# A retention layer and a spatial-gating MLP in one kernel: the order of the first loads, the split of a group's loads, and the engine of one residue

## The chip, the cores and the metric

The kernel runs on one core of one Trainium2 chip. The time is device microseconds (us) of that core for one execution; lower is better. Engines are named as in the profile: PE is TensorE (PEld its weight load), DVE is VectorE, ACT is ScalarE, POOL is GpSimd, SP is SyncE, which here only issues transfers (DMAs).

## The reference

Inputs q, k, v have 4 batches, 8 heads, 768 positions and 64 features per head. The first half is a retention layer, a linear attention with a decay per head; the second an MLP with spatial gating on its output x (4 x 768 x 512):

```
state = gamma[h] * state + outer(k_t, v_t)          # 64 x 64 for each batch and head
y_t   = scale * q_t @ state
x     = y laid out as (batch, position, 8*64)
h     = relu(x @ w_in)                              # 512 -> 1024, u and v are its halves
v_n   = (v - mean(v)) / sqrt(var(v) + 1e-6)         # over the 512 features
v_s   = w_spatial @ v_n + b_spatial                 # over the 768 positions
out   = (u * v_s) @ w_out                           # 512 -> 512
```

## The kernel before, in words

**Precision.** The large products are made from two halves of each operand: a high part, rounded to the fast fp32r format, and a low part, the residue (whole minus high). Each product is three matmuls: high x high, high x low, low x high (`split3`, L348). So every operand needs a rounded copy (an ACT cast) and a residue. A residue is made in one of two ways: by `residue` (L125), one subtraction on DVE or POOL; or by `residue_unit` (L146), in which PE multiplies the whole by the identity, subtracts the high part by a product with minus the identity, all in PSUM, and ACT copies the result out.

**Groups.** The sequence is cut into chunks of 128 positions: 6 chunks in each of 4 batches, 24 groups. `load_group` (G, L224) issues four requests for a group: two of 256 KB that bring q and v (tile `qv`, three buffers), one of 512 KB that brings the keys twice, transposed for the scores and natural for the state update (tile `kk`, two buffers), and one of 256 KB with the decays by which the output is multiplied (tile `qd`, two buffers). POOL then multiplies the values by a decay (L241). `ret_set` (S, L265) of group g updates the state with the natural keys of g and makes the scores of group g+1 with the transposed keys of g+1; in the first batch the state is summed in PSUM (tile `total`) and ACT copies it out (L263); DVE masks the scores (L316). `ret_out` (X, L318) makes the group's output on PE, DVE multiplies it by the decays (tile `xf`, L342), ACT rounds it (L345), POOL makes its residue.

**MLP.** `mlp_v` (V, L359) makes v for a chunk, ACT its relu, DVE mean and variance (`bn_stats`, `bn_aggr`, L380 and L381), and POOL three tiny operations of 128 x 1: add epsilon, the power -0.5, minus mean times that (L382, L383, L385). `mlp_norm` (N, L388) normalises on ACT (L391), rounds on ACT (L392) and makes the residue `vnl`: with `residue_unit` (PE and ACT, tile `run`) for the first UNIT_NORM = 6 chunks, that is the first batch, with DVE afterwards. `item` (I, L472) is one of 8 units of a batch: the u products of the next unit (`mlp_u`), the spatial product (`mlp_spatial`, tile `sp`, which needs all six chunks of v_n of the batch), and the output product of the unit before (`mlp_out`, tile `o`), whose fourth unit writes three outputs to HBM from SP.

**Weights.** `load_double` (L) brings a block of 512 KB of a weight that comes as words of 64 bits, `split_double` (C, L168) splits it with six operations of ACT and DVE and then PE (first four blocks) or POOL. `load_spatial` (K) brings w_spatial, two requests of 768 KB (K0, K2) and four of 192 KB (K4, K5), and `split_spatial` (W) rounds a half row block on ACT and makes its residue on PE and ACT (six) or DVE (six).

**Order.** Four strings name the order in which this work is written: START, FIRST (batch 0's items, with batch 1's retention), REST (twice) and LAST. A number is a block, chunk or group; in FIRST and REST a group number counts from the batch. Within the text the build's scheduler places instructions on each engine by its own estimate of when their inputs are there; an engine then takes its list strictly in that order. Three things are pinned to the written order: all loads on SP's queue (`load`, L122; a load also stays behind an output request written just before it), loads issued by ACT (from the tenth weight block), and, after START, all matmuls. Waits of a request (for a buffer to come free) hold everything behind it on SP.

Of the kernel before, what the change touches and what calls it, by code (L numbers as in the profile page):

```python
# [9 lines left out]
F32 = mybir.dt.float32  # L10
# [6 lines left out]
ALU = mybir.AluOpType  # L17
# [9 lines left out]


START = (
    "v m e L0 G0 C0 L1 L2 S-1 C1 G1 L3 C2 S0 X0 G2 C3 L4 L5 S1 X1 K0 V0 C4 G3 S2 X2 K2 V1 C5 N0 G4 L6 "  # L30
    "S3 X3 V2 N1 G5 W00 W10 K4 K5 S4 X4 V3 N2 W20 W30 B V4 N3 L7 U5 X5 W40 W50 N4 V5 G6 N5 L8"
)
FIRST = (
    "C6 L9 I0 C7 W01 L10 C8 I1 G7 W11 W21 Z5 L11 C9 I2 S6 W31 G8 C10 I3 X6 S7 W41 W51 G9 C11 "
    "I4 X7 S8 G10 I5 X8 S9 G11 I6 X9 S10 G12 V0 V1 I7 X10 S11 N0 V2 N1 V3 N2 G13 X11 V4 N3 V5 N4 O7 "
    "N5"
)
REST = (
    "S0 I0 G2 X0 S1 I1 G3 X1 S2 I2 G4 X2 S3 I3 G5 X3 S4 I4 G6 X4 S5 I5 G7 X5 I6 "
    "V0 V1 I7 N0 V2 N1 V3 N2 V4 N3 V5 N4 O7 N5"  # L40
)
LAST = "I0 I1 I2 I3 I4 I5 I6 I7 O7"
# [4 lines left out]
FIRST_QUEUE = 9  # L47
UNIT_BLOCKS = 4
UNIT_SPATIAL = 6
UNIT_NORM = 6  # L50
RAW_BUFS = 3
KK_BUFS = 2
WARM_UP = 10
QD_BUFS = 2


@with_exitstack
def tile_retention_gmlp(
    ctx: ExitStack,
    tc: tile.TileContext,  # L60
    qv: bass.AP,
    kk: bass.AP,
    w_inv: bass.AP,
    w_inu: bass.AP,
    w_sp: bass.AP,
# [2 lines left out]
    mask: bass.AP,  # L68
    eye: bass.AP,
    vdecay: bass.AP,  # L70
    qdecay: bass.AP,
    out: bass.AP,
):
    nc = tc.nc
    P = 128
    B = out.shape[0]
    NG = kk.shape[0]
    NC = NG // B
    C = P // 2
    D = C  # L80
    NP = kk.shape[2] // (4 * D)
    S = NC * P
    KT = w_inv.shape[1]
    DM = KT * P
# [3 lines left out]
    EPS = 1e-6  # L88
# [3 lines left out]
    rpool = ctx.enter_context(tc.tile_pool(name="ret", bufs=2))  # L92
# [7 lines left out]
    minus_t = wpool.tile([P, P], F32R, name="minus_t")  # L100
    vd_t = wpool.tile([P, NC, 2, NP], F32, name="vd_t")
    bsp_t = wpool.tile([P, S], F32, name="bsp_t")
    mhalf = wpool.tile([P, 1], F32, name="mhalf")
    nc.gpsimd.memset(mhalf, -0.5)

# [11 lines left out]
    def mm(out, lhs, rhs, start, stop, pin=False, shared=False):  # L117
        ins = nc.tensor.matmul(out, lhs, rhs, start=start, stop=stop, skip_group_check=shared)  # L118
        if pin or pinned:
            tc.keep_in_program_order(ins)  # L120

    def load(dst, src):  # L122
        tc.keep_in_program_order(nc.sync.dma_start(dst, src))  # L123

    def residue(eng, out, whole, high):  # L125
        eng.tensor_tensor(out, whole, high.bitcast(F32), ALU.subtract)  # L126
# [19 lines left out]
    def residue_unit(out, high, name, *parts):  # L146

        n = out.shape[-1]
        ps = ps_o.tile([P, DM], F32, tag="o", name=f"ru{name}")
        for k, part in enumerate(parts):  # L150
            mm(ps[:, :n], eye_t, part, start=(k == 0), stop=False)
        mm(ps[:, :n], minus_t, high, start=False, stop=True)
        nc.scalar.copy(out, ps[:, :n])  # L153

    def load_double(i):

        if i >= len(doubles):
            return
        if i < 6:
            tag = ("vnh", "vnl")[i // 3]  # L160
            if i % 3 == 0:
                raws[tag] = mpool.tile([P, 3, DM], I64, tag=tag, name=f"raw{i}", bufs=1)
            raws[i] = raws[tag][:, i % 3]
        else:
            raws[i] = mpool.tile([P, DM], I64, tag="raw", name=f"raw{i}", bufs=RAW_BUFS)[:, :]
        (load if i < FIRST_QUEUE else load_weight)(raws[i], doubles[i][2])

    def split_double(i):  # L168
        hi, lo, _ = doubles[i]
        parts = raws.pop(i).bitcast(I32).rearrange("p (n w) -> p n w", w=2)  # L170
        low, top = parts[:, :, 0], parts[:, :, 1]
        a = rpool.tile([P, DM], F32, tag="xf", name=f"da{i}")
        f = mpool.tile([P, DM], F32, tag="u", name=f"df{i}", bufs=3)
        ai, fi = a[:, :].bitcast(I32), f[:, :].bitcast(I32)
        nc.scalar.activation(a, top.bitcast(F32), AF.Abs)
        nc.vector.tensor_scalar(a, a, TOP_MAX, TOP_MIN, ALU.min, ALU.max)
        nc.vector.tensor_scalar(ai, ai, 0x07FFFFFF, 3, ALU.bitwise_and, ALU.logical_shift_left)
        nc.vector.scalar_tensor_tensor(fi, top, -0x40000000, ai, ALU.bitwise_and, ALU.bitwise_or)  # L178
        nc.vector.tensor_scalar(ai, fi, -0x800000, None, ALU.bitwise_and)
        nc.vector.scalar_tensor_tensor(a, low.bitcast(U32), 2.0**-52, a, ALU.mult, ALU.mult)  # L180
        nc.scalar.copy(hi, f)
        if i < UNIT_BLOCKS:
            residue_unit(lo, hi, f"d{i}", f, a)
        else:
            residue(nc.gpsimd, f, f, hi)
            nc.gpsimd.tensor_tensor(lo, f, a, ALU.add)  # L186
# [30 lines left out]
    queries = {}  # L217
    keys = {}
    naturals = {}
    values = {}  # L220
    decays = {}
    xhalf = {}

    def load_group(g):  # L224
        if g >= NG:
            return

        t = rpool.tile([P, 4, 2, NP, C], F32, tag="qv", name=f"qv{g}", bufs=3)
        kt = rpool.tile([P, 2, 2, NP, C], F32, tag="kk", name=f"kk{g}", bufs=KK_BUFS)
        qd = rpool.tile([P, NP, P], F32, tag="qd", name=f"qd{g}", bufs=QD_BUFS)  # L230
        for r in range(2):
            rows = t[ROWS[r], 2 * r : 2 * r + 2]
            load(rows.rearrange("p s i h c -> p (s i h c)"), qv[g, r])
        load(kt[:, :, :, :, :].rearrange("p s i h c -> p (s i h c)"), kk[g])
        load(qd, qdecay[g % NC])
        queries[g], keys[g], naturals[g] = (t[:, 2], t[:, 1]), kt[:, 0], kt[:, 1]
        values[g], decays[g] = (t[:, 0], t[:, 3]), qd
        for r in range(2):
            vd = vd_t[ROWS[r], g % NC].unsqueeze(3).broadcast_to([D, 2, NP, D])
            w = values[g][r][ROWS[r]]  # L240
            nc.gpsimd.tensor_tensor(w, w, vd, ALU.mult)  # L241

    total = {}

    def ret_total(g, i, pin):

        if not total:
            total[0] = ps_o.tile([P, NP, D], F32, tag="o", name="total")
        w = values[g]
# [15 lines left out]
    def ret_set(g, scores=True, update=True):  # L265

        nxt = scores and g + 1 < NG
        upd = [update and g >= 0, update and g >= 0 and g % NC < NC - 1]  # L270
# [77 lines left out]
    def split3(pairs, ps):  # L348
        n = len(pairs)
        i = 0  # L350
        for (ah, al), (bh, bl) in pairs:
            for l, r in ((ah, bh), (ah, bl), (al, bh)):
                mm(ps, l, r, start=(i == 0), stop=(i == 3 * n - 1))
                i += 1
# [4 lines left out]
    def mlp_v(b, c):  # L359
        if c == 0:  # L360
            vn[b] = (
                mpool.tile([P, NC, DM], F32R, tag="vnh", name=f"vnh{b}", bufs=1),
                mpool.tile([P, NC, DM], F32R, tag="vnl", name=f"vnl{b}", bufs=1),
            )
        xh, xl = xhalf[b, c // TT]
        cols = slice((c % TT) * P, (c % TT) * P + P)
        ps = ps_m.tile([P, DM], F32, tag="m", name=f"v{b}_{c}")
        split3(
            [
                ((xh[:, k, cols], xl[:, k, cols]), (winv_h[:, k], winv_l[:, k]))  # L370
                for k in range(KT)
            ],
            ps,
        )
        v = mpool.tile([P, DM], F32, tag="v", bufs=3, name=f"vr{b}_{c}")
        st = mpool.tile([P, 6], F32, tag="bst", bufs=2, name=f"bst{b}_{c}")
        mv = mpool.tile([P, 2], F32, tag="mv", bufs=3, name=f"mv{b}_{c}")
        rs = mpool.tile([P, 1], F32, tag="rs", bufs=3, name=f"rs{b}_{c}")
        nc.scalar.activation(v, ps, AF.Relu)  # L379
        nc.vector.bn_stats(st, v)  # L380
        nc.vector.bn_aggr(mv, st)  # L381
        nc.gpsimd.tensor_scalar(rs, mv[:, 1:2], EPS, None, ALU.add)  # L382
        nc.gpsimd.tensor_tensor(rs, rs, mhalf, ALU.pow)  # L383
        nb = mpool.tile([P, 1], F32, tag="nb", bufs=3, name=f"nb{b}_{c}")
        nc.gpsimd.tensor_scalar(nb, mv[:, 0:1], rs, -1.0, ALU.mult, ALU.mult)  # L385
        norm[b, c] = (v, nb, rs)

    def mlp_norm(b, c):  # L388
        vh, vl = vn[b]
        v, nb, rs = norm.pop((b, c))  # L390
        nc.scalar.activation(v, v, AF.Identity, bias=nb, scale=rs)  # L391
        nc.scalar.copy(vh[:, c], v)  # L392
        if b * NC + c < UNIT_NORM:
            residue_unit(vl[:, c], vh[:, c], f"n{b}_{c}", v)
        else:
            residue(nc.vector, vl[:, c], v, vh[:, c])

    gate = {}
    us = {}
# [72 lines left out]
    def item(b, i):  # L472
# [11 lines left out]
        "U": lambda b, g, n: ret_set(g + n, scores=False),  # L484
        "X": lambda b, g, n: ret_out(g + n),
        "G": lambda b, g, n: load_group(g + n),
        "L": lambda b, g, n: load_double(n),
        "C": lambda b, g, n: split_double(n),
        "W": lambda b, g, n: split_spatial(n // 10, n % 10),
# [98 lines left out]
```

## Time and profile before

| | |
|---|---|
| median of 3 runs | 446.26 us (445.85 to 450.62) |
| the profiled execution | 446.94 us, of it 445.2 us from the first to the last instruction (the span) |
| mean granted TensorE clock | 0.967 of full speed |
| bytes moved | 47.51 MB, mean 107 GB/s |

The profile shows one execution. Busy time of an engine is the time covered by its instructions. In the views, a line `L118 PE MATMUL run<-vr,eye_t` is the matmul helper at line 118 that writes tile `run` from tiles `vr` and `eye_t`; at the end of a line of the order in time, `[4.15 <-ACT winv_w L153]` says that the engine had been idle for 4.15 us and that the last thing it waited for was ACT's instruction of line 153 that writes `winv_w`. A row of the table by stretches gives, for a stretch from A to B, busy time of each engine with its number of instructions, then the granted PE clock, the busy share of the DMA engines and GB/s.

The span has three parts: START up to about 97 us, where the first u product of batch 0 begins; the items of batch 0 (FIRST) up to about 200 us; and batches 1 to 3.

### The profile page before, as it was taken

To read this page: it belongs to the slowest core of one execution; us is meant where nothing else is said; L and a number is where in the kernel's file an instruction comes from. 1 tells how busy PE (TensorE), PEld (TensorE's weight loads), DVE (VectorE), ACT (ScalarE), POOL (GpSimd) and SP (SyncE) were. 2 spreads that over 40 slices of the span, in tenths; PEclk is the share of its full clock that TensorE was granted. 3 is DMA by queue.
4 is the path that set the end of the run, shared out by engine and by line. 5 is a ranking of instruction groups with operands and counts; after the bars stand their busy time and mean duration, and the time that the engine had idled before them with its cause. 6 is when DMAs were issued, how large, how long until landed. Compare 5 with 4: busy or idle time off the path is not lost.

```text
span 445.2 us, 9212 instructions
## 1 busy us (share of the span) xinstructions
PE 404.7 (91%) x3842; PEld 345.3 (78%) x3842; DVE 201.4 (45%) x385; ACT 143.2 (32%) x268; POOL 164.5 (37%) x196
## 2 busy tenths in 40 slices
PE   3886799849997999899999499999999999999996
PEld 1354567539896988679998398889899988999995
DVE  2764933525955565437555212455555124322122
ACT  2343765623222214352112012471113124610312
POOL 2133864535635444433452522325442223210100
PEclk9998899969998999989999699999999999999999
DMA  7965878301123453407451810036432000100101
GB/s 216 266 211 150 271 242 252 117 5 47 49 80 135 144 155 84 143 35 198 134 157 47 250 39 0 0 105 180 121 119 96 2 0 2 71 1 0 71 1 71
DMA packets 17561, 47.51 MB, mean 107 GB/s; under 512 B 2544, under 2 KB 3440, under 8 KB 17520
## 3 DMA queue, kind: packets, MB, share of 16 engines
q1 hardware_dynamic: 17088, 45.35, 33.6%
q10 hardware_dynamic: 432, 1.57, 1.1%
q8 instruction: 30, 0.49, 0.5%
q14 instruction: 11, 0.09, 0.1%
HBM read 40.62 MB, written 6.29 MB: 105 GB/s over the span
## 4 chain that ended last, share of the span: by engine, by line
PE 78%; DMA 7%; DVE 5%; POOL 4%; ACT 3%; issue 2%; SPq 1%; ACTq 0%; DVEq 0%; POOLq 0%
PE sp L118 22%; PE u L118 16%; PE o L118 15%; PE v L118 13%; PE s L118 5%; PE x L118 4%; DMA wst<-in_w_sp_dram 3%; PE rud L118 2%; DMA qv<-in_qv_dram 1%; DMA raw<-in_w_inv_dram 1%; PE run L118 1%; POOL qv L241 1%; DMA kk<-in_kk_dram 1%; SPq L123 1%; DVE df L178 1%
## 5 line engine op out<-in xcount | busy, mean ns | idle before, releaser
L241 POOL TENSOR_TENSOR qv<-qv,vd_t 64x512 f32<-64x512 f32 x48 | 51.1, 1064 | 79.6 <-DMA qv<-in_qv_dram 70.0
L118 PE MATMUL u<-xh,winu_w 128*128 128x384 f32 x256 | 72.9, 348 | 0.0
L126 POOL TENSOR_TENSOR gl<-t,gh 128x384 fp32r<-128x384 f32 x31 | 31.7, 1023 | 106.6 <-ACT gh L442 104.9
L118 PE MATMUL v<-winv_w,xh 128*128 128x512 f32 x192 | 63.5, 412 | 5.7 <-ACT winv_w L153 4.1
L118 PE MATMUL sp<-wsp_h,vnl 128*128 128x384 f32 x192 | 64.2, 334 | 0.0
L118 PE MATMUL sp<-wsp_h,vnh 128*128 128x384 f32 x192 | 64.2, 334 | 0.0
L118 PE MATMUL sp<-wsp_l,vnh 128*128 128x384 f32 x192 | 64.2, 334 | 0.0
L118 PE MATMUL o<-wout_w,gh 128*128 128x512 f32 x192 | 61.3, 400 | 2.5 <-POOL wout_w L186 2.5
L440 DVE TENSOR_TENSOR t<-sp,bsp_t 128x384 f32<-128x384 f32 (+1 forms) x34 | 17.9, 533 | 100.6 <-PE sp L118 100.6
L118 PEld LDWEIGHTS u<-xh,winu_w 128*128 128x128 f32 x256 | 48.0, 193 | 2.1 <-issue 0.5
L118 PEld LDWEIGHTS v<-winv_w,xh 128*128 128x128 f32 x192 | 36.6, 194 | 14.5 <-ACT winv_w L153 4.3
L442 ACT CAST gh<-t 128x384 fp32r<-128x384 f32 (+1 forms) x34 | 16.6, 493 | 92.4 <-DVE t L441 92.2
L316 DVE TENSOR_TENSOR qv<-s,mask_t 64x256 f32<-64x256 f32 x92 | 38.6, 420 | 11.6 <-PE s L118 10.4
L118 PE MATMUL u<-xl,winu_w 128*128 128x384 f32 x128 | 43.6, 341 | 0.0
L118 PEld LDWEIGHTS o<-wout_w,gh 128*128 128x128 f32 x192 | 36.3, 191 | 8.9 <-POOL wout_w L186 2.9
L126 POOL TENSOR_TENSOR xl<-xf,xh 128x512 fp32r<-128x512 f32 x24 | 31.8, 1323 | 30.3 <-ACT xh L345 30.2
L118 PE MATMUL v<-winv_w,xl 128*128 128x512 f32 x96 | 38.9, 406 | 0.8 <-POOL xl L126 0.6
L118 PE MATMUL o<-wout_w,gl 128*128 128x512 f32 x96 | 38.3, 399 | 0.0
L380 DVE BATCH_NORM_STATS2 bst<-vr 128x6 f32<-128x512 f32 x24 | 16.7, 694 | 46.1 <-ACT vr L379 46.1
L118 PEld LDWEIGHTS sp<-wsp_l,vnh 128*128 128x128 f32 x192 | 36.0, 188 | 0.2
L118 PEld LDWEIGHTS sp<-wsp_h,vnh 128*128 128x128 f32 x192 | 36.0, 188 | 0.2
L118 PEld LDWEIGHTS sp<-wsp_h,vnl 128*128 128x128 f32 x192 | 36.0, 188 | 0.0
(75 smaller groups left out, 557.1 us busy)
## 6 DMA issues: line engine op xcount, KB each, us to landing
qv<-in_qv_dram SPq DMA_DIRECT2D x48, 256.0 KB, 4.8
kk<-in_kk_dram SPq DMA_DIRECT2D x24, 512.0 KB, 4.7
qd<-in_qdecay_dram SPq DMA_DIRECT2D x24, 256.0 KB, 2.8
out_dram<-ot SPq DMA_DIRECT2D x23, 256.0 KB, 2.1
raw<-in_w_inv_dram SPq DMA_DIRECT2D x4, 512.0 KB, 8.6
raw<-in_w_inu_dram SPq DMA_DIRECT2D x4, 512.0 KB, 5.7
wst<-in_w_sp_dram SPq DMA_DIRECT2D x2, 768.0 KB, 7.3
raw<-in_w_out_dram ACTq DMA_DIRECT2D x3, 512.0 KB, 3.8
```

The source lines that it names most:

```text
L118: ins = nc.tensor.matmul(out, lhs, rhs, start=start, stop=stop, skip_group_check=shared)
L123: tc.keep_in_program_order(nc.sync.dma_start(dst, src))
L126: eng.tensor_tensor(out, whole, high.bitcast(F32), ALU.subtract)
L178: nc.vector.scalar_tensor_tensor(fi, top, -0x40000000, ai, ALU.bitwise_and, ALU.bitwise_or)
L241: nc.gpsimd.tensor_tensor(w, w, vd, ALU.mult)
L316: nc.vector.tensor_tensor(m[r][ROWS[r], i], ts[i][col, 0], mk, ALU.mult)
L380: nc.vector.bn_stats(st, v)
L440: nc.vector.tensor_tensor(t[:, c], pp[:, c], bsp_t[:, tc_], ALU.add)
L442: nc.scalar.copy(gh[:, c], t[:, c])
```

## The change

The keys are no longer one tile. The transposed keys (`kt`, 256 KB, two buffers) stay in `load_group`, and a new function brings natural keys and decays together in one request of 512 KB (`kd`, two buffers). The new action D is written behind the output X of the group two back, whose buffer it takes. In START the weight requests L3 to L8, and K0, K2, K4, K5 stand earlier than before with respect to the groups' requests that wait. The residue of the normalised chunks is made on DVE in all batches (UNIT_NORM is gone), and of the three tiny operations per chunk the first and the last move from POOL to DVE; the power stays on POOL.

```diff
 START = (
-    "v m e L0 G0 C0 L1 L2 S-1 C1 G1 L3 C2 S0 X0 G2 C3 L4 L5 S1 X1 K0 V0 C4 G3 S2 X2 K2 V1 C5 N0 G4 L6 "
-    "S3 X3 V2 N1 G5 W00 W10 K4 K5 S4 X4 V3 N2 W20 W30 B V4 N3 L7 U5 X5 W40 W50 N4 V5 G6 N5 L8"
+    "v m e L0 G0 D0 C0 L1 L2 S-1 C1 G1 L3 C2 L4 D1 S0 X0 C3 L5 G2 K0 K2 D2 G3 S1 X1 V0 C4 K4 K5 L6 "
+    "D3 G4 S2 X2 V1 C5 N0 B L7 D4 G5 S3 X3 V2 N1 W00 W10 L8 D5 S4 X4 V3 N2 W20 W30 V4 N3 U5 X5 "
+    "W40 W50 N4 V5 G6 D6 N5"
 )
 FIRST = (
-    "C6 L9 I0 C7 W01 L10 C8 I1 G7 W11 W21 Z5 L11 C9 I2 S6 W31 G8 C10 I3 X6 S7 W41 W51 G9 C11 "
-    "I4 X7 S8 G10 I5 X8 S9 G11 I6 X9 S10 G12 V0 V1 I7 X10 S11 N0 V2 N1 V3 N2 G13 X11 V4 N3 V5 N4 O7 "
-    "N5"
+    "C6 L9 I0 C7 W01 L10 C8 I1 G7 W11 W21 Z5 L11 C9 I2 S6 W31 D7 G8 C10 I3 X6 S7 W41 W51 D8 G9 C11 "
+    "I4 X7 S8 D9 G10 I5 X8 S9 D10 G11 I6 X9 S10 D11 G12 V0 V1 I7 X10 S11 D12 N0 V2 N1 V3 N2 G13 X11 "
+    "D13 V4 N3 V5 N4 O7 N5"
 )
 REST = (
-    "S0 I0 G2 X0 S1 I1 G3 X1 S2 I2 G4 X2 S3 I3 G5 X3 S4 I4 G6 X4 S5 I5 G7 X5 I6 "
+    "S0 I0 G2 X0 S1 D2 I1 G3 X1 S2 D3 I2 G4 X2 S3 D4 I3 G5 X3 S4 D5 I4 G6 X4 S5 D6 I5 G7 X5 D7 I6 "
     "V0 V1 I7 N0 V2 N1 V3 N2 V4 N3 V5 N4 O7 N5"
 )
...
         t = rpool.tile([P, 4, 2, NP, C], F32, tag="qv", name=f"qv{g}", bufs=3)
-        kt = rpool.tile([P, 2, 2, NP, C], F32, tag="kk", name=f"kk{g}", bufs=KK_BUFS)
-        qd = rpool.tile([P, NP, P], F32, tag="qd", name=f"qd{g}", bufs=QD_BUFS)
+        kt = rpool.tile([P, 2, NP, C], F32, tag="kt", name=f"kt{g}", bufs=2)
...
-        load(kt[:, :, :, :, :].rearrange("p s i h c -> p (s i h c)"), kk[g])
-        load(qd, qdecay[g % NC])
-        queries[g], keys[g], naturals[g] = (t[:, 2], t[:, 1]), kt[:, 0], kt[:, 1]
-        values[g], decays[g] = (t[:, 0], t[:, 3]), qd
+        load(kt, kT[g])
+        queries[g], keys[g] = (t[:, 2], t[:, 1]), kt
+        values[g] = (t[:, 0], t[:, 3])
...
+    def load_natural(g):
+        if g >= NG:
+            return
+        t = rpool.tile([P, 2, 2 * NP * C], F32, tag="kd", name=f"kd{g}", bufs=2)
+        load(t[:, :, :].rearrange("p s n -> p (s n)"), kd[g])
+        naturals[g] = t[:, 0].rearrange("p (i h d) -> p i h d", i=2, h=NP)
+        decays[g] = t[:, 1].rearrange("p (h n) -> p h n", h=NP)
...
-        nc.gpsimd.tensor_scalar(rs, mv[:, 1:2], EPS, None, ALU.add)
+        nc.vector.tensor_scalar(rs, mv[:, 1:2], EPS, None, ALU.add)
         nc.gpsimd.tensor_tensor(rs, rs, mhalf, ALU.pow)
         nb = mpool.tile([P, 1], F32, tag="nb", bufs=3, name=f"nb{b}_{c}")
-        nc.gpsimd.tensor_scalar(nb, mv[:, 0:1], rs, -1.0, ALU.mult, ALU.mult)
+        nc.vector.tensor_scalar(nb, mv[:, 0:1], rs, -1.0, ALU.mult, ALU.mult)
...
-        if b * NC + c < UNIT_NORM:
-            residue_unit(vl[:, c], vh[:, c], f"n{b}_{c}", v)
-        else:
-            residue(nc.vector, vl[:, c], v, vh[:, c])
+        residue(nc.vector, vl[:, c], v, vh[:, c])
```

The host lays `kT` and `kd` out to match; sizes and buffers of a group add up to the same bytes as before.

More of the change, by code (lines that the diff above doesn't have):

```diff
@@ L49 @@
 UNIT_SPATIAL = 6
-UNIT_NORM = 6
 RAW_BUFS = 3
-KK_BUFS = 2
 WARM_UP = 10
-QD_BUFS = 2
 @with_exitstack
@@ L61, in tile_retention_gmlp @@
     qv: bass.AP,
-    kk: bass.AP,
+    kT: bass.AP,
+    kd: bass.AP,
     w_inv: bass.AP,
@@ L70, in tile_retention_gmlp @@
     vdecay: bass.AP,
-    qdecay: bass.AP,
     out: bass.AP,
@@ L76, in tile_retention_gmlp @@
     B = out.shape[0]
-    NG = kk.shape[0]
+    NG = kT.shape[0]
     NC = NG // B
@@ L80, in tile_retention_gmlp @@
     D = C
-    NP = kk.shape[2] // (4 * D)
+    NP = kT.shape[3]
     S = NC * P
@@ L486, in tile_retention_gmlp @@
         "G": lambda b, g, n: load_group(g + n),
+        "D": lambda b, g, n: load_natural(g + n),
         "L": lambda b, g, n: load_double(n),
@@ L559 @@
         .reshape(B * NC, 2, C, -1),
-        "kk": np.concatenate([transposed(k, True), natural(k)], 3).reshape(B * NC, P, -1),
+        "kT": transposed(k, True).reshape(B * NC, P, 2, NP, C),
+        "kd": np.concatenate(
+            [natural(k).reshape(B * NC, P, -1), np.tile(qd.reshape(NC, P, -1), (B, 1, 1))], 2
+        ).astype(np.float32),
         "w_inv": words(moe_w_in[:, DM:]),
@@ L568 @@
         "vdecay": vdecay.astype(np.float32),
-        "qdecay": qd.astype(np.float32),
     }
```

## The prediction

> **What bounds the kernel now.** I read the page first: which engine is full, and over the whole span.
>
> ```profile
> span 445.2 us, 9212 instructions
> PE 404.7 (91%) x3842; PEld 345.3 (78%) x3842; DVE 201.4 (45%) x385; ACT 143.2 (32%) x268; POOL 164.5 (37%) x196
> ```
>
> PE is idle for 445.2 - 404.7 = 40.5 us. Where is that? The table by stretches of 10 us (busy us of PE, PEld, DVE, ACT, POOL; granted clock, DMA share, GB/s) answers:
>
> ```profile
> 10.00:20.00 10.00, 7.82 (x42) 3.19 (x42) 7.86 (x15) 3.03 (x5) 2.79 (x3) 1.00 1.04 315
> 40.00:50.00 10.00, 6.80 (x95) 5.47 (x96) 9.60 (x16) 6.04 (x15) 6.59 (x7) 0.70 0.61 199
> 60.00:70.00 10.00, 9.00 (x115) 5.79 (x114) 4.23 (x9) 7.50 (x16) 4.13 (x7) 1.00 0.90 271
> 70.00:80.00 10.00, 10.00 (x59) 6.36 (x57) 1.53 (x4) 5.21 (x10) 6.49 (x8) 1.00 0.70 221
> 200.00:210.00 10.00, 10.00 (x141) 9.55 (x141) 7.23 (x16) 2.93 (x8) 4.34 (x4) 1.00 0.70 203
> ```
>
> From about 200 us on PE is full at full clock: the batches after the first are bound by PE's work, which the change leaves alone. START is another regime: early it waits (6.80 of 10 us at 0.70 clock between 40 and 50), later PE is full there too (10.00 between 70 and 80). So I read START closely. First SP's queue, in order of time:
>
> ```profile
> 11.28 1.76 SPq L123 DMA_DIRECT2D qv<-in_qv_dram  x2
> 25.00 0.33 SPq L123 DMA_DIRECT2D kk<-in_kk_dram  x1
> 28.29 0.43 SPq L123 DMA_DIRECT2D wst<-in_w_sp_dram  x1
> 42.42 0.33 SPq L123 DMA_DIRECT2D qd<-in_qdecay_dram  x1
> 42.80 0.42 SPq L123 DMA_DIRECT2D wst<-in_w_sp_dram  x1
> ```
>
> Group 2's keys wait from 13.0 until 25.00 for the buffer of group 0, and L4, L5 and K0 stand behind them although they need no such buffer; K2 stands behind the decays of group 3 until 42.80. What follows from K0's late issue is in the order of time of ACT, PE and DVE:
>
> ```profile
> 38.26 1.75 ACT L211 CAST wsp_h<-wst 128x384 fp32r<-128x384 f32 x4 [6.57 <-DMA wst<-in_w_sp_dram]
> 40.54 0.72 PE L118 MATMUL v<-winv_w,xh 128*128 128x512 f32 x1 [4.15 <-ACT winv_w L153]
> 41.72 0.68 DVE L342 TENSOR_TENSOR xf<-x,qd 128x512 f32<-128x512 f32 x1
> ```
>
> ACT's list has the rounding of w_spatial ahead of the copy that finishes a weight block for V0; it waits 6.57 us for the transfer, and PE 4.15 us for ACT. Last the end of START:
>
> ```profile
> 87.16 0.39 PE L118 MATMUL v<-winv_w,xl 128*128 128x512 f32 x1
> 88.94 0.18 DVE L381 BATCH_NORM_AGGREGATE mv<-bst 128x2 f32<-128x6 f32 x1
> 89.20 1.04 POOL L241 TENSOR_TENSOR qv<-qv,vd_t 64x512 f32<-64x512 f32 x1
> 90.32 1.26 POOL L186 TENSOR_TENSOR winu_w<-df,da 128x512 fp32r<-128x512 f32 x1
> 93.87 0.81 ACT L391 ACTIVATE vr<-vr,nb,rs 128x512 f32<-128x512 f32 x1 [1.60 <-POOL nb L385]
> 94.74 2.08 PE L118 MATMUL run<-vr,eye_t 128*128 128x512 f32 x2 [7.20 <-ACT vr L391]
> 97.04 0.52 PE L118 MATMUL u<-xh,winu_w 128*128 128x384 f32 x1
> 101.97 0.33 PE L118 MATMUL sp<-wsp_h,vnh 128*128 128x384 f32 x1
> ```
>
> V5 ends at 87.55. Its mean and variance are there at 89.12, but the small operations stand on POOL behind 2.4 us of other work; then the last residue runs on PE (`run`), ahead of the u products on PE's list, and PE stands idle 7.20 us although u's inputs have long been there.
>
> **The change part by part.**
>
> *The last chunk's residue on DVE.* It no longer stands on PE before u. The u products (97.04 to 101.97, 4.9 us, some of it still at low clock) can run while V5 is normalised, and only `sp` waits for the residue. The new chain after 89.12 is priced from rows of this trace:
>
> ```profile
> 80.20 0.18 DVE L381 BATCH_NORM_AGGREGATE mv<-bst 128x2 f32<-128x6 f32 x1
> 81.58 0.69 DVE L342 TENSOR_TENSOR xf<-x,qd 128x512 f32<-128x512 f32 x1 [1.20 <-PE x L118]
> 81.86 0.81 ACT L391 ACTIVATE vr<-vr,nb,rs 128x512 f32<-128x512 f32 x1
> L391 ACT ACTIVATE vr<-vr,nb,rs 128x512 f32<-128x512 f32 x24 | 19.5, 812 | 17.1 <-POOL nb L385 17.1
> L392 ACT CAST vnh<-vr 128x512 fp32r<-128x512 f32 x24 | 14.9, 622 | 3.7 <-PE sp L118 3.4
> L126 DVE TENSOR_TENSOR vnl<-vr,vnh 128x512 fp32r<-128x512 f32 x18 | 12.4, 691 | 17.1 <-ACT vnh L392 17.1
> ```
>
> With nothing in its way the three small operations take 81.86 - 80.38 = 1.5 us. Two of them on DVE have no row; DVE's own small operation takes 0.18, so between 0 and 0.2 us each, and one more change of engine: 1.7 us. Then 0.81 + 0.62 + 0.69 = 2.1 us: `sp` could start at 89.12 + 1.7 + 2.1 = 92.9, against 101.97, a gain of 9.0. If the power on POOL still stands behind those 2.4 us, 6.6. I take 7.6.
>
> *The other five.* Each costs PE what the chain of waits shows of one while it is warm:
>
> ```profile
> 71.76 1.09 PE run L118 x3
> ```
>
> 5 x 1.1 = 5.5 us, on a PE that is 90 to 100% busy there (rows 60 and 70): 5.0 us off the path. If another engine set the pace, 0. DVE gets 6 x 0.69 = 4.1 us more in START; it was busy 4.23 and 1.53 us of those 10, so I count it as covered; uncovered, each residue shows once, 4.1 us at most. ACT loses six copies, which I count at nothing.
>
> On that cover the Trainium skill says, in "SBUF — State Buffer", section "SBUF: two separate sides", that a DVE operation with two SBUF inputs and a GpSimd operation that reads SBUF lock each other out of a shared port for a whole instruction. The trace has it for a DVE operation of one input:
>
> ```profile
> 83.27 1.68 POOL L126 TENSOR_TENSOR xl<-xf,xh 128x512 fp32r<-128x512 f32 x1 [1.44 <-ACT xh L345]
> 83.83 1.40 DVE L179 TENSOR_SCALAR da<-df 128x512 int32<-128x512 int32 x1
> 93.82 0.43 DVE L179 TENSOR_SCALAR da<-df 128x512 int32<-128x512 int32 x1
> ```
>
> 1.40 us beside POOL, 0.43 alone. By the rule each moved residue may take 1 us longer, and only the last is on the path: the sum would be 1 us worse.
>
> *Weight requests ahead.* K0 and K2 now stand before group 2's natural keys and group 3, the only requests that wait there. The 4.15 us of PE's wait go, and with them the low clock after it: 6.80 us busy at 0.70 is 2.0 us lost. If ACT waits as long somewhere else, 0; both gone, 6.2. I take 6.2 here and a charge for new waits below.
>
> *Groups' data earlier.* START needs 7 x 1280 KB of groups, 9 x 512 of weights, 2304 of w_spatial and 504 others (from the shapes in the code), 16.8 MB. At 315 GB/s (row 10) that is 53 us, at 271 (row 60) 62, at 199 (row 40) 84. I take 62: with L3 to K2 not held, the queue does not run dry, for natural keys and decays of group g wait only for X of g-2, and there are 1.5 MB of other requests before it at the first such wait. So X5 could come near 60 us instead of 81.6 (xf, above); but PE's list then sets the end. Of PE's remaining idle time before 50 us (3.2 of it in row 40, where part follows the stall) I take 2.0 as won, between 0 and 5.
>
> *Natural keys and decays together, later.* In the later batches 256 KB more stand before the next group's q and v on SP, 0.9 us at 271 to 315 GB/s. Where POOL's multiplication of q and v is close to the path (wout_w near 138 us, batch 1's first normalised chunk near 184 us) that may cost 0.9 each, or nothing: I take both, 1.8. Before group 18's scores it helps:
>
> ```profile
> 246.96 0.54 SPq L123 DMA_DIRECT2D kk<-in_kk_dram  x1
> 249.32 2.15 POOL L241 TENSOR_TENSOR qv<-qv,vd_t 64x512 f32<-64x512 f32 x2 [1.34 <-DMA qv<-in_qv_dram]
> 251.69 1.97 PE L118 MATMUL s<-qv,kk 64*64 64x64 f32 x48 [6.49 <-DMA kk<-in_kk_dram]
> ```
>
> The request stays behind three outputs, so the wait stays; but from q and v landed (249.3) to keys landed took 2.3 us for 512 KB, and 256 KB need half: 1.2 us won.
>
> *New waits.* Every list is new, and set by estimates. A wait like ACT's 6.57 us can return elsewhere: 0 to 6.6, I take 4. Also the second small DVE operation waits for POOL's power, and all of DVE behind it; that is the rival below.
>
> *Sum.* -7.6 - 5.0 - 6.2 - 2.0 + 1.8 - 1.2 + 4.0 = -16.2. Against this execution's own time, 446.94 us (span 445.2 and 1.7 around it), 430.7; against the median of the runs, 446.26, which is 0.7 lower, **430 us**.
>
> **The rivals.**
>
> *More: START is paced by its data.* If no list stalls, START ends with the last group's data at 62 us and about 12 us for X5, V5 and the chain above: `sp` at 75 instead of 102, 27 us, so 419. For it: DMA idle while SP waits. Against it: PE had 10.00 of 10 us to do between 70 and 80. By sum without new waits it is 426.
>
> *Less: the wait moves, the rest stays.* ACT's list again has a rounding of w_spatial before its data: K0 and K2 end 8.2 MB into the stream, at 271 GB/s near 30 us, and now every early engine waits for them. Then the 6.2 and 2.0 are not won, and of the 12.6 us on PE some 9 remain: 437.
>
> *It doesn't do what it says.* Weight blocks 7 to 11 are split on DVE and POOL alongside the items. The output product of the second unit starts at 118.4 on a block that POOL ended at 118.05:
>
> ```profile
> 105.29 0.56 DVE L440 TENSOR_TENSOR t<-sp,bsp_t 128x384 f32<-128x384 f32 x1 [10.31 <-PE sp L118]
> 116.77 1.28 POOL L186 TENSOR_TENSOR wout_w<-df,da 128x512 fp32r<-128x512 f32 x1 [0.70 <-DVE da L180]
> 118.39 0.62 PE L118 MATMUL o<-wout_w,gh 128*128 128x512 f32 x2
> ```
>
> If that chain is set by its own work and not by START's end, all that START wins is waited off there: no change, 446. Against it: DVE is idle between 95 and 105 us, and block 8's buffer comes free with the first unit's product, so the chain moves with the items.
>
> *Slower: DVE stops behind POOL.* In the waits by pairs POOL waits for q and v more than for anything but its residues:
>
> ```profile
> POOL qv L241 <- DMA qv<-in_qv_dram: 70.0, 25, 9.4
> ```
>
> The power stands in POOL's list among those multiplications; DVE now waits for it, and masks, outputs and splits wait behind DVE. If the 24 waits average the 2.8 us of that row, DVE stands 67 us. It decides when more than 16 of these fall where PE waits for a mask or an output; at a third of them, 22, the time is 452. Against it: between 70 and 80 us DVE is busy 1.53 of 10, so a stop there costs little.
>
> **How the numbers follow.** Forecast, 424 to 434: 0.46. Less, 434 to 441.5: 0.24. More, 414 to 424: 0.14. No change: 0.08. Slower: 0.08. The range 418 to 444 leaves out the lower part of "more" (0.04), two thirds of "no change" and "slower": 0.17. A measurement of this kernel tells about 1%, 4.5 us: faster by more than that is 0.46 + 0.24 + 0.14 = 0.84, within 0.08, slower 0.08.
>
> **What would show it.** Right: wst issued before 20 us and no idle time of PE over 4 us between 30 and 50; no `run` tile; u starting directly after V5 and `sp` first at about 85 instead of 102; the stretch from that point to the end within 2 us of before (343 us); PE still full after 200 us. Wrong: `sp` first later than 95; POOL's power late and DVE idle before the operation of line 385 (by the old numbering); output products waiting for wout_w by more than the 2.5 us of before.

## The result

The changed kernel takes 431.84 us (median of 4 runs, 431.24 to 432.87) beside 448.44 for the kernel before (4 runs, 445.85 to 452.44): a ratio of 0.9625, 95% interval 0.9536 to 0.9713. In a later set of runs it was 433.0 beside 449.33, 0.9678 (0.9607 to 0.9749). Medians hold all runs, ratios leave out the few that fell in a slower state of the chip (one of the four behind 433.0, at 438.01). The forecast was 430, range 418 to 444. The profiled execution of the changed kernel took 432.38 us, span 430.6.

First its page:

```profile
span 430.6 us, 9138 instructions
PE 395.7 (92%) x3824; PEld 341.9 (79%) x3824; DVE 219.4 (51%) x439; ACT 139.1 (32%) x262; POOL 152.0 (35%) x148
```

18 matmuls fewer (the six `run` triples), 54 DVE instructions more, 48 POOL instructions fewer: the change is there. The stretches of START:

```profile
30.00:40.00 10.00, 10.00 (x68) 6.86 (x65) 8.76 (x16) 8.07 (x19) 3.68 (x3) 1.00 1.05 298
50.00:60.00 10.00, 6.74 (x95) 4.95 (x95) 9.74 (x12) 4.46 (x11) 6.86 (x5) 0.98 0.48 149
60.00:70.00 10.00, 9.65 (x93) 7.65 (x94) 4.76 (x13) 5.37 (x11) 5.15 (x5) 0.67 0.85 224
70.00:80.00 10.00, 6.17 (x40) 4.28 (x35) 5.37 (x12) 4.61 (x8) 5.46 (x6) 0.84 0.53 144
```

The early wait is gone: PE is full between 30 and 40 us (its wait of 4.15 us ended at 40.54 before). But between 50 and 60 us DVE is now the full engine, 9.74 of 10, and PE has 6.74; between 70 and 80 PE has 6.17 at 0.84 clock where it was full at 1.00. SP's queue in order of time shows both halves of the reordering:

```profile
17.84 1.61 SPq L122 DMA_DIRECT2D wst<-in_w_sp_dram  x2
26.58 0.33 SPq L122 DMA_DIRECT2D kd<-in_kd_dram  x1
35.73 0.35 SPq L122 DMA_DIRECT2D kd<-in_kd_dram  x1
47.79 0.33 SPq L122 DMA_DIRECT2D kd<-in_kd_dram  x1
60.32 0.33 SPq L122 DMA_DIRECT2D kd<-in_kd_dram  x1
```

Both large requests for w_spatial leave by 19.5 us (28.29 and 42.80 before). Natural keys and decays (`kd`) of groups 2 to 5 still leave only after the output of two groups back is made. The end of START, in order of time of PE, DVE and POOL:

```profile
82.27 0.63 PE L117 MATMUL v<-winv_w,xl 128*128 128x512 f32 x1
82.70 0.52 PE L117 MATMUL u<-xh,winu_w 128*128 128x384 f32 x1
86.30 0.18 DVE L386 BATCH_NORM_AGGREGATE mv<-bst 128x2 f32<-128x6 f32 x1
86.75 0.55 POOL L388 TENSOR_TENSOR rs<-rs,mhalf 128x1 f32<-128x1 f32 x1 [1.64 <-DVE rs L387]
89.73 1.71 DVE L125 TENSOR_TENSOR vnl<-vr,vnh 128x512 fp32r<-128x512 f32 x1
91.50 0.44 PE L117 MATMUL sp<-wsp_h,vnl 128*128 128x384 f32 x1 [1.11 <-DVE vnl L125]
```

u begins as soon as V5 is through, and the spatial product runs until it needs the last chunk's residue; it waits 1.11 us. Before, PE stood 7.20 us here.

Five marks in PE's order of time divide the span of both executions:

| from ... to | before, us | after, us | difference | forecast | after, a second execution |
|---|---|---|---|---|---|
| start ... V5's last matmul ends | 87.55 | 82.90 | -4.7 | -9.2 (-5.0 -6.2 -2.0 +4.0) | 80.43 |
| ... third u product (batch 0) starts | 17.54 | 8.87 | -8.7 | -7.6 | 8.29 |
| ... fourth output product has its weights | 34.57 | 34.94 | +0.4 | +0.9 | 37.86 |
| ... group 18's scores start | 112.03 | 109.30 | -2.7 | +0.9 -1.2 | 109.58 |
| ... end | 193.51 | 194.59 | +1.1 | 0 | 193.44 |
| span | 445.2 | 430.6 | -14.6 | -16.2 | 429.6 |

The sum is right and its first row is not. Two executions of the same changed kernel differ by 2 to 3 us in the first row and in the third, so a smaller difference in a single row says little. The two differences are of opposite sign: what START won more in the second execution, PE waited off at the fourth output product, whose weight block came no sooner (the execution above first, then the second):

```profile
126.71 0.50 PE L117 MATMUL o<-wout_w,gh 128*128 128x512 f32 x1 [2.86 <-POOL wout_w L185]
126.58 0.80 PE L117 MATMUL o<-wout_w,gh 128*128 128x512 f32 x1 [4.88 <-POOL wout_w L185]
```

The experiments say what the first row consists of.

### The profile page after: what moved, and what is told of

It is laid out like the page before. It is cut to its first block, busy times and chain, and to the rows that moved or that the text cites. A ratio compares the mean times of both kernels' runs of the same rounds, so it can differ in the third digit from the quotient of the medians.

```text
span 430.6 us, 9138 instructions
## 1 busy us (share of the span) xinstructions
PE 395.7 (92%) x3824; PEld 341.9 (79%) x3824; DVE 219.4 (51%) x439; ACT 139.1 (32%) x262; POOL 152.0 (35%) x148
## 4 chain that ended last, share of the span: by engine, by line
PE 68%; DMA 10%; DVE 10%; ACT 4%; POOL 4%; issue 3%; SPq 1%; ACTq 0%; POOLq 0%; DVEq 0%
PE sp L117 21%; PE u L117 14%; PE o L117 14%; PE v L117 8%; PE x L117 5%; DMA qv<-in_qv_dram 5%; PE s L117 4%; DMA kd<-in_kd_dram 2%; POOL qv L238 2%; DVE vnl L125 2%; DMA raw<-in_w_inv_dram 1%; DVE da L179 1%; DVE qv L321 1%; DVE da L175 1%; DMA kt<-in_kT_dram 1%
## 5 line engine op out<-in xcount | busy, mean ns | idle before, releaser
L238 POOL TENSOR_TENSOR qv<-qv,vd_t 64x512 f32<-64x512 f32 x48 | 52.3, 1090 | 88.2 <-DMA qv<-in_qv_dram 85.4
L117 PEld LDWEIGHTS x<-qv 128*64 128x64 f32 (+1 forms) x768 | 27.5, 144 | 12.9 <-issue 7.6
```

## The experiments

The kernel before ran again beside each set: 451.17, 449.83 and 449.33 us. Ratios are to these.

**n_only: the last part of the change alone.** In the kernel before:

```diff
-        if b * NC + c < UNIT_NORM:
-            residue_unit(vl[:, c], vh[:, c], f"n{b}_{c}", v)
-        else:
-            residue(nc.vector, vl[:, c], v, vh[:, c])
+        residue(nc.vector, vl[:, c], v, vh[:, c])
...
-        nc.gpsimd.tensor_scalar(rs, mv[:, 1:2], EPS, None, ALU.add)
+        nc.vector.tensor_scalar(rs, mv[:, 1:2], EPS, None, ALU.add)
...
-        nc.gpsimd.tensor_scalar(nb, mv[:, 0:1], rs, -1.0, ALU.mult, ALU.mult)
+        nc.vector.tensor_scalar(nb, mv[:, 0:1], rs, -1.0, ALU.mult, ALU.mult)
```

> The kernel before, with only the last part of the change: residues of normalised chunks on DVE in all batches, and the first and last small operation on DVE. My theory: the tail of START goes (-8) and the five other products on PE give part of their 5.5 us, but the chunk residues crowd DVE: 434 to 440, with at least 7 us less between the end of V5's matmuls and the third unit's u product, and at most 4 us won before V5 ends. Rival, that the order of the requests makes the gain: 444 or more.

438.74 us, ratio 0.9729 (0.9661 to 0.9798). From V5's end to the third u product 7.85 us instead of 17.54: the tail is this part's. V5 itself ends at 92.06, not earlier than the 87.55 of before. The rival, that the order makes all of the gain, falls.

**order_only: the other part alone.** The changed kernel with that diff turned round.

> The changed kernel with the last part undone: six residues on PE and ACT, the three small operations on POOL; order and split of the requests as changed. My theory: the tail stays (17 us from the end of V5 to the third unit's u product, as before), and the order alone gives 3 to 8: 438 to 444. Rival, that the order makes the gain: 434 or less.

441.0 us, ratio 0.9804 (0.9736 to 0.9873). The tail is back, 17.70 us, with the same rows:

```profile
82.20 1.26 POOL L185 TENSOR_TENSOR winu_w<-df,da 128x512 fp32r<-128x512 f32 x1
83.55 0.22 POOL L387 TENSOR_SCALAR rs<-mv 128x1 f32<-128x1 f32 x1
86.62 2.07 PE L117 MATMUL run<-vr,eye_t 128*128 128x512 f32 x2 [6.48 <-ACT vr L396]
88.92 0.52 PE L117 MATMUL u<-xh,winu_w 128*128 128x384 f32 x1
```

V5 ends at 80.14. So the order wins 7.4 us up to there, where its terms in my sum came to 4.2 (-6.2 - 2.0 + 4.0), and 8.8 in all by the ratio (5.7 to 11.9 by its interval), where the sum had 3.6 (with +0.6 later). And putting the five earlier residues on DVE as well does not bring V5 forward: 80.14 with all six on PE, 80.4 to 84.0 in the six profiled executions that have this START and all residues on DVE. By the spans of the profiled executions the two parts add up to the whole: -8.6 (n_only) and -6.7 (order_only), -14.6 and -15.6 for both together.

**tiny_pool: the three small operations back on POOL, residues on DVE.**

```diff
-        nc.vector.tensor_scalar(rs, mv[:, 1:2], EPS, None, ALU.add)
+        nc.gpsimd.tensor_scalar(rs, mv[:, 1:2], EPS, None, ALU.add)
...
-        nc.vector.tensor_scalar(nb, mv[:, 0:1], rs, -1.0, ALU.mult, ALU.mult)
+        nc.gpsimd.tensor_scalar(nb, mv[:, 0:1], rs, -1.0, ALU.mult, ALU.mult)
```

> The changed kernel with the three small operations back on POOL, residues on DVE. Theory: DVE's 18.3 us of waiting for POOL's power are hidden, so 430 to 434, no difference that 1% shows. Rival, that DVE stopping behind POOL costs START: 427 or less. Second rival, that three operations behind POOL's multiplications cost more than one: 435 or more.

431.13 us, 0.9544 (0.9464 to 0.9625): as the changed kernel. The mechanism of my slower rival does exist, in the waits by pairs of the changed kernel:

```profile
DVE nb L390 <- POOL rs L388: 18.3, 15, 3.5
```

18.3 us in 15 waits, not the 67 that I feared, and taking them away changes nothing that can be measured.

**last_on_dve: five residues on PE again, the sixth on DVE.** In the changed kernel:

```diff
-        residue(nc.vector, vl[:, c], v, vh[:, c])
+        if b * NC + c < 5:
+            residue_unit(vl[:, c], vh[:, c], f"n{b}_{c}", v)
+        else:
+            residue(nc.vector, vl[:, c], v, vh[:, c])
```

> The changed kernel with the first five chunk residues of batch 0 on PE and ACT again and only the sixth on DVE. Theory: before V5, DVE sets the pace (two residues of 3.02 us together stand in front of an output at 59.63), so moving five residues off it brings V5's end from 82.9 to about 80 (80.1 where all six were on PE), and the tail of 9 us stays: 2 to 3 us faster than the changed kernel, 427 to 430. Rival, my step on record that PE sets the pace there: V5 ends 5 us later than in the changed kernel, 435 or more.

V5 ends at 80.09, as the theory has it, the tail is 7.30 us, and the third u product starts at 87.39, 4.4 us before that of the changed kernel. But the time is 431.22, 0.9586 (0.951 to 0.9662), outside the 427 to 430 that I gave: what was won is lost later. PE waits 3.69 us for the last weight block (2.86 in the changed kernel) and 2.48 us near 173 us for the first V products of the next batch (0.62), and behind these waits it runs at 0.66 clock between 120 and 130 us and 0.88 between 170 and 180 (0.90 and 1.00). The rival, that V5 comes 5 us later with 5 triples more on PE, falls. The stretches of this kernel:

```profile
50.00:60.00 10.00, 10.00 (x127) 6.81 (x128) 5.26 (x11) 6.50 (x14) 8.48 (x8) 0.93 0.80 232
70.00:80.00 10.00, 9.93 (x62) 6.34 (x62) 6.96 (x12) 7.14 (x14) 4.20 (x4) 1.00 0.41 109
```

PE is full again, at 0.93 and 1.00 clock, and DVE has 5.26 instead of 9.74; V5's end is no later than in the changed kernel. What the residues do on DVE is seen in the changed kernel's order of time of DVE, POOL and PE:

```profile
56.09 3.02 DVE L125 TENSOR_TENSOR vnl<-vr,vnh 128x512 fp32r<-128x512 f32 x2
56.96 1.59 POOL L185 TENSOR_TENSOR winu_w<-df,da 128x512 fp32r<-128x512 f32 x1
59.63 0.67 DVE L347 TENSOR_TENSOR xf<-x,kd 128x512 f32<-128x512 f32 x1
60.35 1.52 PE L117 MATMUL x<-qv 128*64 128x64 f32 x18 [2.88 <-DVE xf L347]
```

An output waits behind two residues, and PE waits 2.88 us for that output. But this delay is not what holds V5. V5 needs the last group's output. In order of time of DVE, ACT and PE that output and V5's first product, in the changed kernel and then in order_only:

```profile
73.50 0.68 DVE L347 TENSOR_TENSOR xf<-x,kd 128x512 f32<-128x512 f32 x1
75.95 0.60 ACT L350 CAST xh<-xf 128x512 fp32r<-128x512 f32 x1
76.60 1.11 PE L117 MATMUL v<-winv_w,xh 128*128 128x512 f32 x2 [3.27 <-ACT xh L350]
...
74.07 0.69 DVE L347 TENSOR_TENSOR xf<-x,kd 128x512 f32<-128x512 f32 x1 [1.37 <-POOL rs L388]
75.28 0.61 ACT L350 CAST xh<-xf 128x512 fp32r<-128x512 f32 x1
76.11 1.03 PE L117 MATMUL v<-winv_w,xh 128*128 128x512 f32 x2
```

The output is there at about the same time with the residues on DVE or on PE, and V5 starts at about the same time. With the residues on PE, its list has work up to V5 (tiles `ruw` and `run`); without them it stands idle. All six executions with every residue on DVE have a wait of 3.06 to 5.17 us there, none of the three with five or six on PE has one over 1 us.

**weights_only and split_only: the two halves of the order.** The first is the kernel before with START's weight requests ahead, the second the changed kernel with residues and small operations as before, START's requests where they stood, and each D directly behind its G:

```diff
 START = (   # weights_only
+    "v m e L0 G0 C0 L1 L2 S-1 C1 G1 L3 C2 L4 L5 K0 K2 S0 X0 C3 G2 G3 S1 X1 V0 C4 K4 K5 L6 "
+    "G4 S2 X2 V1 C5 N0 B L7 G5 S3 X3 V2 N1 W00 W10 L8 S4 X4 V3 N2 W20 W30 V4 N3 U5 X5 "
+    "W40 W50 N4 V5 G6 N5"
 START = (   # split_only
+    "v m e L0 G0 D0 C0 L1 L2 S-1 C1 G1 D1 L3 C2 S0 X0 G2 D2 C3 L4 L5 S1 X1 K0 V0 C4 G3 D3 S2 X2 K2 V1 C5 N0 G4 D4 L6 "
+    "S3 X3 V2 N1 G5 D5 W00 W10 K4 K5 S4 X4 V3 N2 W20 W30 B V4 N3 L7 U5 X5 W40 W50 N4 V5 G6 D6 N5 L8"
```

> The kernel before, keys and decays as before and residues as before, with only START's weight requests written ahead of the groups' requests that wait. Theory: this is the larger part of what the order gave (V5 ending at 80.1 instead of 87.6): V5 ends at 80 to 84, 441 to 446 beside 451 for the kernel before. Rival, that the split of keys and decays is what lets the queue run on: V5 ends at 86 or later, 448 or more.

> Keys and decays split as in the changed kernel, but each group's second request directly behind the first and START's weight requests where they stood before; residues and small operations as before. Theory: the natural keys with the decays wait for the output of two groups back just as the decays did, so START gains little: V5 ends at 86 to 89, 447 or more beside 451. Rival, that the split is the gain: V5 ends at 82 or sooner, 443 or less.

446.17 us, 0.991 (0.9863 to 0.9956), V5's end at 83.84; and 444.51 us, 0.9884 (0.9804 to 0.9963), V5's end at 84.66. The first falls just outside its 441 to 446, though V5 ends where I said. My theory of the second half was wrong, and its rival does not fit either: the split alone wins about as much as the weights alone. It lets the transposed keys of group 2 leave without waiting for the buffer of group 0's natural ones, and group 1's output is made at 30.62 instead of 41.72; that this is the mechanism is argued, not tried by itself (this kernel has the changed FIRST and REST too). 0.9% and 1.2% add up to about the 2.0% of the whole order; neither is larger beyond the intervals.

**g6_first: the loads of group 6 ahead of three outputs.** In REST of the changed kernel:

```diff
-... S4 D5 I4 G6 X4 S5 D6 ...
+... S4 D5 G6 I4 X4 S5 D6 ...
```

> The changed kernel with group 6's loads of a REST batch written before the fourth unit instead of behind its three outputs. Theory: the 6.33 us in which PE waits for the transposed keys near 230 us go, and the low clock behind them: 423 to 427, and no wait over 1 us of PE there. Rival, that the wait only changes its cause (POOL's multiplication, a buffer that is not free): 430 or more.

424.5 us, 0.9414 (0.9341 to 0.9487). The wait was one that my prediction had seen and that the change left: in the changed kernel, in order of time of SP, POOL and PE,

```profile
231.06 0.58 SPq L122 DMA_DIRECT2D kt<-in_kT_dram  x1
233.58 2.15 POOL L238 TENSOR_TENSOR qv<-qv,vd_t 64x512 f32<-64x512 f32 x2 [1.11 <-DMA qv<-in_qv_dram]
236.01 0.50 PE L117 MATMUL s<-qv,kt 64*64 64x64 f32 x6 [6.33 <-DMA kt<-in_kT_dram]
```

and in this one, its queue and its stretch:

```profile
221.69 0.58 SPq L122 DMA_DIRECT2D kt<-in_kT_dram  x1
225.71 1.92 SPq L469 DMA_DIRECT2D out_dram<-ot  x3
```

```profile
230.00:240.00 10.00, 10.00 (x82) 9.27 (x81) 2.90 (x6) 2.12 (x4) 4.73 (x5) 1.00 0.54 144
```

PE is full at 1.00 clock where it had 3.99 of 10 at 0.69 (shown at the end). By the medians that is 7 to 9 us from one word moved, by the ratios to the kernel before 9 to 12.

**c11_first and g6_sum_dve: the wait for the last weight block.** Both on top of g6_first. The first writes the split of the last weight block ahead of D8 and G9 (`S7 C11 W41 W51 D8 G9 I4`); the second instead makes that block's last sum on DVE:

```diff
-            nc.gpsimd.tensor_tensor(lo, f, a, ALU.add)
+            pick(i == 11).tensor_tensor(lo, f, a, ALU.add)
```

> The changed kernel with group 6's loads ahead of the fourth unit (424.5 by itself) and, in the first batch's items, the split of the last weight block written ahead of the requests for group 8 and 9. Theory: PE's wait of 2.9 to 4.7 us for that block's low half, which stands behind POOL's multiplication of group 9's q and v, goes: 420 to 422.5. Rival: DVE and ACT reach the block no sooner, because its buffers come free with the unit before: 424 or more, and the wait stays over 2 us.

> The changed kernel with group 6's loads ahead of the fourth unit, and the last sum of the last weight block (its low half) on DVE instead of POOL. Theory: that sum stood behind POOL's multiplication of group 9's q and v; on DVE it follows its own input at once, so PE's wait before the output product falls from 3.7 us to under 1: 420 to 422.5, beside 424.5 without it. Rival, that the block's inputs are what is late: wait still over 2 us, 424 or more.

The first: 424.46 us, 0.9431 (0.9369 to 0.9493), and PE still waits 3.80 us; my theory fails. The time is the one that its rival names, for another reason. The order of time of POOL and PE in it shows the sum still behind the multiplication, which waits for its data:

```profile
124.56 2.15 POOL L238 TENSOR_TENSOR qv<-qv,vd_t 64x512 f32<-64x512 f32 x2 [1.40 <-DMA qv<-in_qv_dram]
126.79 1.46 POOL L185 TENSOR_TENSOR wout_w<-df,da 128x512 fp32r<-128x512 f32 x1
128.30 0.50 PE L117 MATMUL o<-wout_w,gh 128*128 128x512 f32 x1 [3.80 <-POOL wout_w L185]
```

The second: 422.2 us, 0.9403 (0.9366 to 0.944), inside its 420 to 422.5 but not to be told from g6_first, with a wait of 2.78. Its sum now stands behind DVE's masks and takes 1.47 us beside POOL (126.04 to 127.51). The wait only changed its engine; that half of my theory fails too.

**changed_again and all_three.** The changed kernel once more, beside the last two, and g6_first, g6_sum_dve and last_on_dve together:

> The changed kernel as it is, for comparison on the chip of the two beside it: 0.96 of the kernel before, as first measured (0.954 to 0.971).

> The same, and the first five chunk residues of batch 0 on PE again. Theory: what the one alone won by the first output product (2.7 us) adds if no wait is set anew later: 417 to 421. Rival: as there, the later lists take it back: 421 to 424.

433.0 us (above) and 421.11 us, 0.9377 (0.9342 to 0.9411), at the border of the two expectations. It is the lowest median of these kernels. By its interval it beats last_on_dve; those of g6_first and g6_sum_dve overlap with its own.

## Why the prediction was right, point by point

- **The tail** (-7.6): measured -8.7, and -8.8 between order_only and the changed kernel (17.70 and 8.87). The mechanism is the one forecast: `run` no longer stands before u, and PE works while the last chunk is normalised. By the ratios the whole last part, given the order, is 5.7 to 8.0 us, so the tail accounts for all of it.
- **The other five** (-5.0 "on a PE that is 90 to 100% busy there"): this step failed. I took PE's full stretches for the pace. V5 waits for the last group's output, which DVE makes at 73.50 us in the changed kernel and at 74.07 with all six residues on PE, and it starts at 76.60 and at 76.11. The time taken off PE came back as idle time (6.17 of 10 at 0.84 clock between 70 and 80): a wait of 3.06 to 5.17 us, and V5's products behind it at half pace, so that V5 ends at 82.90 instead of 80.14. Part of the wait is ACT's: it rounds that output 1.8 us after it is there, behind four other operations (0.5 us in order_only). What sets the time of the last output was not tried. That DVE had room for five more residues was wrong as well: "uncovered, each residue shows once, 4.1 us at most" was the bound that I kept and should have weighed, for I read DVE's free time between 60 and 80 us and not between 40 and 50, where the row showed it at 9.60 of 10; an output at 59.63 now waits behind two of them. That delay is not seen in the last output.
- **The order** (-6.2 - 2.0 + 4.0 and +0.6 later, together -3.6): 7.4 us by V5's end and 8.8 by the ratio (interval 5.7 to 11.9). The stall of 4.15 us went. The new waits that I charged 4.0 for came: order_only has two, of 1.89 and 1.74 us before 45 us, and between 40 and 50 us its clock is as low (0.73) as before the change (0.70). The term that was too small is that of the earlier data (-2.0): between 10 and 40 us PE's idle time falls from 8.6 to 2.2 us, more than the stall. By themselves the weights ahead bring V5's end 3.7 us forward and the split 2.9; in the sum the split had a share of that -2.0 at most.
- By V5's end the first error is +5 to +8 us and the second -3. They cancel in part; most of what is left, +2 to +4.5, is made good by a tail that won 1.1 to 1.7 us more than forecast and by 2 us in the fourth row that the sum did not have. The total was right for a reason that is half luck.
- **Group 18's keys** (-1.2): mis-sized. The request is half as large, but from q and v landed to keys landed it still took 2.4 us (233.58 to 236.01), and PE's wait is 6.33 instead of 6.49. Three more requests left right behind it (one of 512 KB and two of 256 KB, 231.73 to 233.33), in a stretch in which the DMA engines were 0.94 busy; that they shared its time was not tried by itself.
- **Later multiplications** (+1.8): +0.4 at the weight block; near 180 us the changed kernel waits less than before (1.2 us against 2.2), order_only and last_on_dve, with the same loads, 3.0 and 3.1. All seven executions with every residue on DVE wait 0.2 to 1.4 us there, all six with five or six of them on PE 1.9 to 3.9: so this gain, with the clock behind the wait (1.00 between 165 and 205 us, 0.96 before the change) most of the -2.7 in the fourth row, goes with the move of the residues and was not in the sum. Why was not tried.
- **The rivals.** "It doesn't do what it says", the weight chain in the items, is true in part: that stretch took 34.9 us beside 34.6 in one execution and 37.9 in the other, where PE waits 4.88 us for the last block, so some of what START wins beyond this is waited off there. "DVE stops behind POOL" is real and small. "More" had `sp` first at 75 us; it comes at 87.28 and 84.96.

## What to carry to other kernels

An engine that a page shows full is the pace only if taking work from it brings the next stage sooner: look for what the next stage waits for in the same stretch, here the last group's output and its way through DVE and ACT, before counting freed time as won. A residue or any helper that only the last consumer needs should not stand in an in-order list before work that is ready. And a prefetch written behind the store of a result inherits that result's wait.

## What the runs showed of the hardware

Work taken off PE left it waiting, and behind the wait it ran at a lower clock. In the changed kernel's order of time of PE, around the wait before V5:

```profile
71.20 0.61 PE L117 MATMUL v<-winv_w,xh 128*128 128x512 f32 x2
71.65 0.39 PE L117 MATMUL v<-winv_w,xl 128*128 128x512 f32 x1
71.88 0.61 PE L117 MATMUL v<-winv_w,xh 128*128 128x512 f32 x2
...
76.60 1.11 PE L117 MATMUL v<-winv_w,xh 128*128 128x512 f32 x2 [3.27 <-ACT xh L350]
78.86 1.05 PE L117 MATMUL v<-winv_w,xh 128*128 128x512 f32 x2
79.71 0.63 PE L117 MATMUL v<-winv_w,xl 128*128 128x512 f32 x1
80.14 1.05 PE L117 MATMUL v<-winv_w,xh 128*128 128x512 f32 x2
```

Three matmuls take 0.68 us before the wait (71.20 to 71.88) and 1.28 after it (78.86 to 80.14). The same is seen around the wait for group 18:

```profile
230.00:240.00 10.00, 3.99 (x54) 3.90 (x55) 2.55 (x7) 0.62 (x1) 3.61 (x4) 0.69 0.94 255
```

The Trainium skill says in "TensorE: Matmul & The Clock Gate", Part 1, that the clock halves after about 3.4 us without activity and returns after as long a busy time. The wait of 6.33 us agrees. Those of 3.27 us and of 2.88 us (60.35, above) are shorter than that, and matmuls ran at half pace behind them too (clock 0.67 between 60 and 70 us), so here a shorter wait is enough. V5's twelve products behind the wait at 76.60 stand 0.43 us apart instead of 0.23: an estimate of 2.4 us that this wait costs beyond itself.

The six residues that went to DVE brought the mean of its residues of normalised chunks from 691 to 849 ns:

```profile
L125 DVE TENSOR_TENSOR vnl<-vr,vnh 128x512 fp32r<-128x512 f32 x24 | 20.1, 849 | 7.8 <-ACT vnh L397 7.7
```

Two of them beside POOL took 3.02 us (56.09, above), where 2 x 0.69 is their time alone. That agrees with the rule of the shared port that the prediction cites from the Trainium skill, and it met four of the six (1.5 to 1.8 us each instead of 0.69), not only the last. The other two, at 63.16 and 75.61, fell where POOL was idle and took 0.69 and 0.68.
